# A fused Fourier filter and MLP on one core: twiddles put into the first and last DFT tables, and batch 0 worked by channel halves with most of its last stage in later slots

## The chip, the cores and the metric

The kernel runs on one core of a Trainium2 chip. The metric is device time in microseconds (us) from one launch; the time given for a kernel is the median of several runs on the same chip. Engines are named as in the profile: PE (TensorE), DVE (VectorE), ACT (ScalarE), POOL (GpSimd) and SP (SyncE, which here only issues DMAs).

## The reference, cut to what matters

```python
# x: 8 x 3008 x 256, filt_r and filt_i: 1505 x 256, w_in: 256 x 2048, w_out: 2048 x 256
X = np.fft.rfft(x, axis=1)
y = np.fft.irfft(X * (filt_r + 1j * filt_i)[None], n=3008, axis=1)
t = y.reshape(8 * 3008, 256)
h = t @ w_in
out = (0.5 * h * (1 + erf(h / sqrt(2)))) @ w_out
```

## The kernel before, in words

**The Fourier part.** 3008 is 47 x 64. A position n is written 64*n1 + 32*h + w, with n1 of 0..46, h of 0..1 and w of 0..31. Only 24 values k1 of the first transform are computed, since x is real. There are four stages: a DFT over n1 (table T1), a DFT over the 64 values (h, w) with the twiddle of each k1 (table T2), the product with the filter F, the inverse over 64 (T3, and T3i with real and imaginary parts turned), and the inverse over 47 (T4). T2 and T3 hold one 128x128 matrix for each of the 24 k1.

**Batch 0** goes first, alone, on the chip's own memory (functions c1 to c4). c1 multiplies x by T1 (16 groups; each is copied out of PSUM by DVE or ACT, L327 and L325). c1t transposes it to b_sb. c2 multiplies by T2, and DVE multiplies the PSUM result by F into p (L569; the last of the twelve is cut in two, L574). c3 multiplies by T3, and ACT copies it to vt_sb. c3t transposes vt_sb into d_sb (8 copies on DVE), and c4 multiplies by T4c and writes y_sb, the ring that the MLP reads (16 copies, 14 on ACT and 2 on DVE). The tables are made on the way by iotas on POOL, angles on DVE, sines on ACT, and matmuls with eye and swap. Each filter value is needed in both halves of the 128 partitions; dup_filters copies it (L137), two calls on DVE, one on ACT, nine on POOL. warm_up (L319) puts matmuls of ones into PE's queue between the steps.

**Batches 1 to 7** pass through HBM between the stages. fold (L109, L110) makes sums and differences of the two h on DVE, s1 (L429) is stage 1 with one table T1s for all positions, its result goes to R1 in HBM by SP's queue and comes back by r1, s2 (L456) and s2_out (L467) are stage 2 and the filter product with Fu (a second arrangement of F, made by move_filters, L130), s3 (L487) goes to R2, r2 reads it, and s4 (L514) multiplies by T4a. T4a, T2p, U and their factors are made on POOL and PE during the first tiles (table_2_parities, table_u_pick, table_4_rows, weights_4, table_4_factors, table_4_all).

**The MLP** runs over 47 tiles of 512 positions. mm1 (L640) makes 128x512 of h by two matmuls, and ACT applies Gelu into g_sb (L643). mm2 is mm2_first for tiles 0 to 2 (L656) and mm2_seven after that, which does seven products of sums instead of eight (L714; the sums on DVE, L685, L691, L696).

**What sets the order.** Each engine does its instructions in the program's order. After batch 0 the main loop runs over slots, 16 to a tile; slot s issues what was put there by put(slot, ...), then the mm2 matmuls of that slot, then one mm1. Tile 0's mm2_first starts in slot 10, so slots 0 to 9 hold ten mm1 and what is put there (fold in slots 0, 1, 5, 8; s1 in slots 4, 8, 11, 13). PSUM has eight banks: while batch 0 is worked, w (2), m (1) and n (5); in the main loop h (3), o (2) and f (3). An s1 takes three f banks and one lent from o or h. A DMA on POOL's or SP's queue waits for the one eight before it on that queue.

Of the kernel before, what the change touches and what calls it, by code (L numbers as in the profile page):

```python
# [10 lines left out]
ALU = mybir.AluOpType  # L11
# [20 lines left out]
class _Mix:  # L32
    def __init__(self, ctx, tc, x, filt_r, filt_i, w_in, w_out, out):
# [22 lines left out]
        self.T1 = c.tile([2 * NA, 96], BF16, name="T1")  # L56
        self.T2p = c.tile([128, K1, 2, 2, 16], BF16, name="T2p")
        self.xs = c.tile([128, 4, 256], BF16, name="xs")
        self.U = c.tile([128, 2, 2 * HB], BF16, name="U")
        self.T4c = c.tile([96, NA, 2], BF16, name="T4c")  # L60
# [5 lines left out]
        self.T4a = f[0:96, 4096:7168].rearrange("p (w m) -> p w m", w=HB)  # L66
# [54 lines left out]
    def move_filters(self, m0, m):  # L121

        for c in (3, 2, 1, 0):
            for q in range(2):
                for e in range(2):
                    o, k = 32 * c + 16 * q, 6 * c + m0
                    for t in ((0, 1),) if c or m0 == 0 else ((0,), (1,)):
                        t = slice(t[0], t[-1] + 1)
                        i = self.F[32 * q + e:32 * q + 32:2, t, k:k + m, :]
                        self.nc.sync.dma_start(  # L130
                            out=self.Fu[o:o + 16, t, e ^ q, m0:m0 + m, :].rearrange("p t m c -> p t (m c)"),
                            in_=i.rearrange("p t m c -> p t (m c)"))

    def dup_filters(self, eng, k0, k):
        for k in range(k0, k0 + k, 2):
            o, i = (self.F[r:r + 64, :, k:k + 2, :].rearrange("p t a b -> p t (a b)") for r in (64, 0))
            (eng.copy if eng is self.nc.scalar else eng.tensor_copy)(out=o, in_=i)  # L137
# [32 lines left out]
    def table_1(self, g):  # L170

        nc, ts = self.nc, self.nc.vector.tensor_scalar
        col = lambda name: g.tile([128, 1], FP32, name=name)
        off = g.tile([128, 2, K1], FP32, name="off")
        nc.vector.memset(off[:, 0, :], 0.25)
        nc.vector.memset(off[:, 1, :], 0.5)
        h, n1, hs, hc = col("h"), col("n1"), col("hs"), col("hc")
        ts(out=h, in0=self.p, scalar1=float(NA), scalar2=None, op0=ALU.is_ge)
        nc.vector.scalar_tensor_tensor(out=n1, in0=h, scalar=-float(NA), in1=self.p, op0=ALU.mult, op1=ALU.add)
        ts(out=hs, in0=h, scalar1=2.0 * PI, scalar2=None, op0=ALU.mult)  # L180
        ts(out=n1, in0=n1, scalar1=1.0 / NA, scalar2=None, op0=ALU.mult)
        ts(out=hc, in0=h, scalar1=-2.0 * PI, scalar2=2.0 * PI, op0=ALU.mult, op1=ALU.add)
        self.table_2_rows(g)
        w, r = g.tile([128, 2, K1], FP32, name="w1"), g.tile([128, 2, K1], FP32, name="r1")
        nc.vector.scalar_tensor_tensor(out=w, in0=self.k48, scalar=n1, in1=off, op0=ALU.mult, op1=ALU.add)
        ts(out=r, in0=w, scalar1=RND, scalar2=-RND, op0=ALU.add, op1=ALU.add)
        nc.vector.tensor_tensor(out=w, in0=w, in1=r, op=ALU.subtract)
        for q, s in enumerate((hc, hs)):
            nc.scalar.activation(out=self.T1[:, 48 * q:48 * q + 48], in_=w[0:2 * NA].rearrange("p a b -> p (a b)"),
                                 func=AF.Sin, scale=s[0:2 * NA])  # L190

    def table_2_rows(self, g):


        v = self.nc.vector
        ts = v.tensor_scalar
        col = lambda name, dt=FP32: g.tile([128, 1], dt, name=name)
        ri_i, m_i = col("ri_i", I32), col("m_i", I32)
        ts(out=m_i, in0=self.pi, scalar1=1, scalar2=None, op0=ALU.logical_shift_right)
        ts(out=ri_i, in0=self.pi, scalar1=1, scalar2=None, op0=ALU.bitwise_and)  # L200
        self.n2, self.ri = col("n2"), col("ri")
        v.tensor_copy(out=self.n2, in_=m_i)
        v.tensor_copy(out=self.ri, in_=ri_i)
        ts(out=self.n2, in0=self.n2, scalar1=1.0 / self.S, scalar2=None, op0=ALU.mult)
        ts(out=self.ri, in0=self.ri, scalar1=-0.25, scalar2=TURNS + 0.25, op0=ALU.mult, op1=ALU.add)

    def table_2_angle(self, g, h):


        v = self.nc.vector  # L210
        ts = v.tensor_scalar
        w = self.gen
        if h == 0:
            col = lambda name: g.tile([128, 1], FP32, name=name)
            jn = g.tile([128, NB], FP32, name="jn")
            ts(out=jn, in0=self.jj, scalar1=self.n2, scalar2=self.ri, op0=ALU.mult, op1=ALU.add)
            n6, self.n12 = col("n6"), col("n12")
            ts(out=n6, in0=self.n2, scalar1=6.0, scalar2=None, op0=ALU.mult)
            ts(out=self.n12, in0=self.n2, scalar1=12.0, scalar2=None, op0=ALU.mult)
            v.scalar_tensor_tensor(out=w[:, 0:6], in0=self.kk.unsqueeze(2).to_broadcast([128, 6, NB]), scalar=self.n2,  # L220
                                   in1=jn.unsqueeze(1).to_broadcast([128, 6, NB]), op0=ALU.mult, op1=ALU.add)

            self.T1c = g.tile([2 * NA, 96], BF16, name="T1c")
            v.tensor_copy(out=self.T1c.rearrange("p (k h r) -> p k h r", h=2, r=2),
                          in_=self.T1.rearrange("p (h r k) -> p k h r", h=2, r=2))
            ts(out=w[:, 6:12], in0=w[:, 0:6], scalar1=n6, scalar2=None, op0=ALU.add)
        else:
            ts(out=w[:, 12:24], in0=w[:, 0:12], scalar1=self.n12, scalar2=None, op0=ALU.add)
        k = slice(12 * h, 12 * h + 12)
        ts(out=self.gen_s.bitcast(I32), in0=w[:, k].bitcast(I32), scalar1=15, scalar2=None,  # L230
           op0=ALU.logical_shift_left)

    def signs(self, g):

        set_ = self.nc.vector.memset
        self.turn = [g.tile([128, 1], FP32, name=n) for n in ("turn_r", "turn_i")]
        for t, s in zip(self.turn, (-1.0, 1.0)):
            set_(t, s)
            for lo in (32, 96):
                set_(t[lo:lo + 32], -s)  # L240

        self.wtc = g.tile([128, 1], FP32, name="wtc")
        set_(self.wtc, 2.0)
        set_(self.wtc[0:4], 1.0)

    def weights_4(self, g):


        ts = self.nc.gpsimd.tensor_scalar
        h, q, self.wt, self.wts = (g.tile([128, 1], FP32, name=n) for n in ("h48", "q48", "wt", "wts"))  # L250
        ts(out=h, in0=self.p, scalar1=48.0, scalar2=None, op0=ALU.is_ge)
        ts(out=q, in0=h, scalar1=-48.0, scalar2=-4.0, op0=ALU.mult, op1=ALU.add)
        self.nc.gpsimd.tensor_tensor(out=q, in0=self.p, in1=q, op=ALU.add)
        self.nc.gpsimd.tensor_tensor(out=q, in0=q, in1=q, op=ALU.mult)
        ts(out=q, in0=q, scalar1=16.0, scalar2=-1.0, op0=ALU.is_equal, op1=ALU.mult)
        ts(out=self.wt, in0=q, scalar1=2.0, scalar2=None, op0=ALU.add)
        ts(out=h, in0=h, scalar1=-2.0, scalar2=1.0, op0=ALU.mult, op1=ALU.add)
        self.nc.gpsimd.tensor_tensor(out=self.wts, in0=self.wt, in1=h, op=ALU.mult)

    def unit_matrices(self, g, cols):  # L260
        ts = self.nc.vector.tensor_scalar
        self.eye, self.swap = (g.tile([128, 128], BF16, name=n) for n in ("eye", "swap"))
        sg, to = (g.tile([128, 1], FP32, name=n) for n in ("sg", "to"))

        ts(out=sg, in0=self.ri, scalar1=8.0, scalar2=-8.0 * TURNS - 1.0, op0=ALU.mult, op1=ALU.add)
        self.nc.vector.tensor_tensor(out=to, in0=self.p, in1=sg, op=ALU.add)
        ts(out=self.swap, in0=cols, scalar1=to, scalar2=sg, op0=ALU.is_equal, op1=ALU.mult)
        ts(out=self.eye, in0=cols, scalar1=self.p, scalar2=None, op0=ALU.is_equal)

    def table_2_sin(self, h):  # L270
        k = slice(12 * h, 12 * h + 12)
        self.nc.scalar.activation(out=self.T2[:, k, 0, :], in_=self.gen_s.bitcast(I32), func=AF.Sin,
                                  scale=2.0 * PI / 2.0 ** 32)

    def table_2_swap(self, h):
        t2 = self.T2[:, 12 * h:12 * h + 12]
        for i in range(2):
            ps = self.bank("ps_sw", "n")
            self.nc.tensor.matmul(ps[:, 0:384], lhsT=self.swap, rhs=t2[:, :, 0, 32 * i:32 * i + 32],
                                  start=True, stop=True)  # L280
# [760 lines left out]
```

## Time and profile before

| | |
|---|---|
| median of 3 runs | 733.68 us (733.53 to 733.91) |
| span of the profiled execution, first to last instruction | 732.0 us |
| PE busy | 713.6 us (97%) |
| DVE busy | 597.0 us (82%) |
| ACT busy | 576.5 us (79%) |
| POOL busy | 286.2 us (39%) |
| granted TensorE clock | 0.999 mean |
| first mm1 matmul (L640) | 37.30 us |
| first mm2 matmul (L656) | 44.02 us |

The span is what the profile sees of one execution; the runs are timed around it, so they are a little longer (1.7 us here). The profile's timeline gives for each engine the start of a group of like instructions, the time that it covers, the line, the operation with output and input, and how many; a bracket gives idle time before it and what ended it. Busy PE time is modelled, and a busy PE isn't a PE at its peak, but a wait that the view of waits puts on PE is one.

### The profile page before, as it was taken

What the parts mean: (1) busy time and instruction counts of PE and PEld (TensorE: products, weight loads), DVE (VectorE), ACT (ScalarE), POOL (GpSimd) and SP (SyncE); (2) the same over time, 40 slices, a digit from 0 to 9 for tenths busy, and PEclk for the clock granted to TensorE, in tenths of its full rate; (3) what the DMA queues carried; (4) which work ended last, traced back from release to release, by engine and by line L of the source; (5) the groups of instructions that cost most, each with busy time, mean ns of one, the idle gap of its engine ahead of it and who ended that gap; (6) DMA issues with size and microseconds to landing.
All of it is one profiled execution on the core that took longest, in us unless ns stands there. A gap on an engine that the chain in (4) does not pass through costs nothing.

```text
span 732.0 us, 22073 instructions
## 1 busy us (share of the span) xinstructions
PE 713.6 (97%) x9016; PEld 505.9 (69%) x9165; DVE 597.0 (82%) x1091; ACT 576.5 (79%) x1050; POOL 286.2 (39%) x546
## 2 busy tenths in 40 slices
PE   7999999999999999999999999999999999999997
PEld 4846675676777666666677667666677767777776
DVE  8975698899878998798976999779988897775666
ACT  7997778688877888778887788877888788877773
POOL 7853377864223452135511364115531121121121
PEclk9999999999999999999999999999999999999999
DMA  9886544765355553646535455355545442411011
GB/s 158 160 173 161 155 89 123 201 124 100 88 169 143 120 112 107 178 99 134 128 107 162 114 132 119 97 149 151 110 102 135 141 117 84 114 47 42 30 59 59
DMA packets 81254, 87.72 MB, mean 120 GB/s; under 512 B 13393, under 2 KB 61137, under 8 KB 81153
## 3 DMA queue, kind: packets, MB, share of 16 engines
q0 software_dynamic: 22288, 39.50, 24.3%
q1 hardware_dynamic: 58449, 46.62, 23.8%
q8 instruction: 71, 1.16, 0.7%
q14 instruction: 30, 0.25, 0.1%
q10 hardware_dynamic: 416, 0.20, 0.1%
HBM read 54.00 MB, written 46.66 MB: 138 GB/s over the span
## 4 chain that ended last, share of the span: by engine, by line
PE 86%; DVE 4%; DMA 4%; issue 2%; POOL 2%; ACT 1%; DVEq 0%; POOLq 0%; ACTq 0%
PE ps_o L714 38%; PE ps_h L640 38%; PE ps_s L514 3%; PE ps_o L656 2%; PE ps_s L429 2%; PE ps_s L487 2%; DMA x_sb<-in_x_dram 2%; PE ps_s L456 2%; DVE s_sb L685 1%; DMA w_out_sb<-in_moe_w_out_dram 1%; POOL F L137 1%; DMA F<-in_filt_i_dram 1%; ACT g_sb L643 1%; DVE p L467 1%; POOL x_sb L92 1%
## 5 line engine op out<-in xcount | busy, mean ns | idle before, releaser
L643 ACT ACTIVATE g_sb<-ps_h 128x512 f16<-128x512 f32 x752 | 446.4, 601 | 139.9 <-PE ps_h L640 115.5
L640 PE MATMUL ps_h<-y_sb,w_in_sb 128*128 128x512 bf16 (+3 forms) x1455 | 415.0, 365 | 1.5 <-DVE p L467 0.7
L761 POOL DMA_DIRECT2D out_dram<-ost x231 | 131.4, 575 | 388.0 <-DVE ost L743 361.3
L714 PEld LDWEIGHTS <-g_sb 128*128 128x128 f16 x2816 | 184.4, 98 | 80.7 <-issue 14.6
L640 PEld LDWEIGHTS <-w_in_sb 128*128 128x128 bf16 x1600 | 126.3, 98 | 8.3 <-issue 2.4
L714 PE MATMUL ps_o<-w_sums,g_sb 128*128 128x128 f16 x1408 | 121.7, 219 | 1.7 <-DVE g_sb L691 0.2
L714 PE MATMUL ps_o<-w_sums,s_sb 128*128 128x128 f16 x1408 | 121.2, 219 | 1.6
L714 PEld LDWEIGHTS <-s_sb 128*128 128x128 f16 x1408 | 95.1, 98 | 37.6 <-issue 2.5
L685 DVE TENSOR_TENSOR s_sb<-g_sb 128x1024 f16<-128x1024 f16 x176 | 116.4, 692 | 0.4 <-ACT g_sb L643 0.3
L714 PE MATMUL ps_o<-w_out_sb,g_sb 128*128 128x128 f16 x1408 | 113.7, 219 | 1.8
L467 DVE TENSOR_TENSOR p<-ps_s,Fu 128x1024 bf16<-128x1024 f32 x84 | 101.5, 1216 | 9.1 <-PE ps_s L456 6.5
L101 POOL DMA_DIRECT2D x_sb<-in_x_dram x156 | 79.4, 515 | 3.1 <-issue 1.6
L691 DVE TENSOR_TENSOR g_sb<-s_sb,g_sb 128x1024 f16<-128x1024 f16 x88 | 60.3, 687 | 1.5
L714 PE MATMUL ps_o<-w_out_sb,F 128*128 128x128 f16 x704 | 60.6, 219 | 0.9
L696 DVE TENSOR_TENSOR F<-g_sb 128x1024 f16<-128x1024 f16 x88 | 61.4, 697 | 0.0
L714 PEld LDWEIGHTS <-F 128*128 128x128 f16 x704 | 47.1, 98 | 14.6 <-issue 0.4
L736 DVE TENSOR_TENSOR t_sb<-t_sb,ps_o 128x256 f32<-128x256 f32 x44 | 18.4, 417 | 39.0 <-PE ps_o L714 38.6
L514 PEld LDWEIGHTS <-d_sb 96*128 96x128 bf16 x448 | 31.4, 97 | 26.8 <-issue 1.3
L325 ACT ACTIVATE F<-ps_s 128x512 bf16<-128x512 f32 x83 | 45.5, 607 | 0.1
L325 ACT ACTIVATE y_sb<-ps_s 128x376 bf16<-128x376 f32 x95 | 45.4, 478 | 0.1
L327 DVE CAST a_sb<-ps_s 128x512 bf16<-128x512 f32 x54 | 34.7, 684 | 12.0 <-PE ps_s L429 11.7
L743 DVE TENSOR_TENSOR ost<-t_sb,ps_o 128x256 f32<-128x256 f32 x86 | 32.1, 414 | 13.7 <-PE ps_o L714 13.7
(160 smaller groups left out, 589.2 us busy)
## 6 DMA issues: line engine op xcount, KB each, us to landing
out_dram<-ost POOLq DMA_DIRECT2D x127, 128.0 KB, 2.9
b_sb<-R SPq DMA_DIRECT2D x21, 512.0 KB, 5.1
R<-F SPq DMA_DIRECT2D x84, 128.0 KB, 2.5
d_sb<-R SPq DMA_DIRECT2D x56, 192.0 KB, 4.3
R<-a_sb SPq DMA_DIRECT2D x108, 96.0 KB, 2.2
x_sb<-in_x_dram POOLq DMA_DIRECT2D x48, 94.0 KB, 2.7
x_sb<-in_x_dram POOLq DMA_DIRECT2D x48, 48.0 KB, 2.8
x_sb<-in_x_dram POOLq DMA_DIRECT2D x12, 188.0 KB, 5.0
```

Of the source, the lines that this page charges most:

```text
L101: self.nc.gpsimd.dma_start(out=xt[64 * v + to:64 * v + to + m, h, 4 * c:4 * c + 4 * n, :], in_=xv[h][at:at + m, w:w + 4 * n, :])
L325: self.nc.scalar.activation(out=out, in_=in_, func=AF.Copy, scale=1.0 if scale is None else scale)
L327: self.nc.vector.tensor_copy(out=out, in_=in_)
L467: v(out=w[:, a], in0=ps.unsqueeze(2).to_broadcast([128, 2, 2, 256]), in1=f.unsqueeze(1).to_broadcast([128, 2, 2, 256]), op=ALU.mult)
L514: nc.tensor.matmul(ps[:, 94 * i:94 * i + 94], lhsT=d[:, (grp % 2) * 4 + i, 128 * half:128 * half + 128], rhs=self.T4a[:, 4 * grp + i, 0:2 ...
L640: nc.tensor.matmul(ps[:, o:o + n], lhsT=w[:, dc], rhs=self.ring[:, dc, off:off + n], start=(dc == 0), stop=(dc == 1))
L643: nc.scalar.activation(out=self.st["g", t][:, jc, :], in_=ps, func=AF.Gelu)
L685: self.nc.vector.tensor_tensor(out=self.st["s", t][:, i:i + 2], in0=a, in1=b, op=ALU.subtract)
L691: self.nc.vector.tensor_tensor(out=a21[:, k], in0=self.st["s", t][:, k, 0], in1=a22[:, k], op=ALU.add)
L696: self.nc.vector.tensor_tensor(out=self.s4_sb[:, k], in0=a12[:, k], in1=s2[:, k], op=ALU.subtract)
L714: nc.tensor.matmul(ps[:, (m + 1) % 2, sub, :], lhsT=a[:, i, 128 * sub:128 * sub + 128], rhs=b[:, i], start=i == 0, stop=i == 7)
L761: eng.dma_start(out=out, in_=tile_[lo - r0:lo - r0 + n])
```

## The change

The positions' twiddle moves out of the second and third tables into the first and the last. T1 becomes a table for each w (94 x 32 x 96), with the sum and the difference of the two h in it; T2 and T3 become one 128x128 matrix for all k1; T4 is a table for each w (96 x 32 x 94), made by 32 transposes of T1 and used by all batches. T1s (for s1) becomes a table for each of 16 positions, T2p and U are small. So the POOL tables in the first tiles go, s1 is 16 matmuls of 256 columns with 16 weights instead of 8 of 512 columns, R2 is written in pieces of one 256-vector and read by one DMA per part instead of two, and c3 uses one T3 for the eight matmuls of a unit.

Batch 0 is worked in twelve units of four k1 and one channel half. c1t, c2, c3 and c3t are done for each half; all of half 0 is finished first. Of the 16 c4 only four are done before the main loop: (0,0) and (1,0) between the last units, (0,1) and (1,1) right before the loop. The other twelve go to slots 2 to 25, copied out by DVE. Four c3t copies of half 0 are on ACT; of half 1 one is split between DVE and ACT, three are on DVE. dup_filters does two pieces on DVE, one on ACT, five on POOL, and SP sends the last eight k1 by DMA. move_filters is cut in three, the third in slot 28. The Gelu table of ACT is loaded in the middle of c1.

The diff, cut to its core ("-" before, "+" after):

```diff
+    def table_1_angle(self, w, n):
+        self.nc.vector.scalar_tensor_tensor(
+            out=b[:, w], in0=self.ww[:, w].unsqueeze(2).to_broadcast([128, n, K1]), scalar=self.first,
+            in1=self.kk.unsqueeze(1).to_broadcast([128, n, K1]), op0=ALU.add, op1=ALU.mult)
+        for r in range(2):
+            ts(out=a[:, r, w], in0=b[:, w], scalar1=1.0 / self.S, scalar2=TURNS + 0.25 + 0.25 * r,
+               op0=ALU.mult, op1=ALU.add)
+        ts(out=i, in0=i, scalar1=15, scalar2=None, op0=ALU.logical_shift_left)
+    def table_1_sin(self, w, n):
+        self.nc.scalar.activation(out=t, in_=a, func=AF.Sin, scale=2.0 * PI / 2.0 ** 32)
+    def table_1_odd(self, w, n, eng):
+        t = self.T1[:, w:w + n].rearrange("p w k a r -> p a (w k) r")
+        self._evac(t[:, 1], t[:, 0], eng, self.sign[0:2 * NA])
+    def table_3(self):
+        self.nc.tensor.transpose(ps[:, 0:128], self.T2, self.eye)
+        self._evac(self.T3[:, 0], ps[:, 0:128], "act")
+        for r in range(2):
+            self._evac(to[:, r], of[:, 1 - r], "act", self.turn[r])
+    def table_4(self, i, eng):
+        for w in range(8):
+            self.nc.tensor.transpose(ps[0:96, 2 * NA * w:2 * NA * w + 2 * NA],
+                                     self.T1[:, 8 * i + w].rearrange("p k a r -> p (k a r)"), self.eye[0:2 * NA, 0:2 * NA])
+        self._evac(self.T4[:, 8 * i:8 * i + 8, 0:2 * NA], ps[0:96, 0:16 * NA].rearrange("p (w m) -> p w m", w=8),
+                   eng, self.wt[0:96])
...
+    def send_filters(self, k, n):
+        self.nc.sync.dma_start(out=o, in_=i)
...
     def s1(self, b, c):
-        for i in range(2):
+        for i in range(4):
             for d in range(2):
                 for v in range(2):
-                    nc.tensor.matmul(ps[i][v][64 * d:64 * d + 64, :], lhsT=self.T1s[64 * v:64 * v + NA],
-                                     rhs=x[d][64 * v:64 * v + NA, 2 * i:2 * i + 2, :], start=True, stop=True)
+                    nc.tensor.matmul(ps[i // 2][v][64 * d:64 * d + 64, 256 * (i % 2):256 * (i % 2) + 256],
+                                     lhsT=self.T1s[64 * v:64 * v + NA, 4 * c + i],
+                                     rhs=x[d][64 * v:64 * v + NA, i, :], start=True, stop=True)
...
+    def c3(self, h, k, eng):
+        for i in range(4):
+            for t in range(2):
+                self.nc.tensor.matmul(ps[:, 128 * i:128 * i + 128], lhsT=w[:, t, 128 * i:128 * i + 128],
+                                      rhs=self.T3[:, t], start=t == 0, stop=t == 1)
+    def c4(self, u, half, eng, tag):
+        d = self.st[0, "d", half, u // 2]
+        ps = self.bank("ps_c4", tag)
+        for i in range(4):
+            self.nc.tensor.matmul(ps[:, 94 * i:94 * i + 94], lhsT=d[:, 4 * (u % 2) + i, :],
+                                  rhs=self.T4[:, 4 * u + i, 0:2 * NA], start=True, stop=True)
+        self.y_out(0, u, half, ps, eng)
...
+    for w, n in ((0, 8), (8, 8)):
+        m.table_1_angle(w, n)
+        m.table_1_sin(w, n)
+        m.table_1_odd(w, n, act)
+    for c in range(4):
+        for i, (u, h) in enumerate(order if c < 3 else [(0, 0), (1, 0), (0, 1), (1, 1)]):
+            m.c1(2 * c + u, h, (dve if c == 0 or i % 2 else act))
+        if c == 0:
+            m.table_1_angle(16, 16)
+            m.table_1_sin(16, 16)
+            m.table_1_odd(16, 16, dve)
+            m.table_2(g)
+            m.warm_up(3)
+            m.table_4(0, act)
+        if c == 1:
+            m.table_2_sin()
+            m.table_4(1, dve)
+            m.warm_up(2)
+        if c == 2:
+            nc.scalar.activation(out=g.tile([128, 1], FP32, name="warm"), in_=m.p, func=AF.Gelu)
+            m.table_4(2, dve)
+            m.table_4(3, dve)
+            m.warm_up(1)
+    m.dup_filters(nc.vector, 0, 0)
+    m.c1t(0, 0, (dve, act))
+    m.dup_filters(nc.scalar, 0, 4)
+    m.dup_filters(nc.vector, 1, 0)
...
+    m.c2(0, 0)
+    m.table_3()
+    m.c1t(1, 0, (act,))
+    m.c2(1, 0)
+    units = [(0, 0), (1, 0), (0, 4), (1, 4), (0, 8), (1, 8), (0, 12), (1, 12), (0, 16), (0, 20), (1, 16), (1, 20)]
+    turns = {0: (0, 8), 2: (1, 8), 5: (0, 16), 7: (1, 16)}
+    for i, (h, k) in enumerate(units):
+        if i in turns:
+            m.c1t(*turns[i], (act,))
+        if i + 2 < 12:
+            m.c2(*units[i + 2])
+        if i < 10:
+            m.warm_up(2)
+        m.c3(h, k, (act,) if i < 11 else (dve, act))
+        if i in (9, 10):
+            for j in range(2):
+                m.c3t(0, 2 * (i - 9) + j, (act,))
+            m.c4(0, 0, act, "n") if i == 9 else m.c4(1, 0, act, "n")
...
+    m.c3t(1, 0, (dve, act))
+    m.c3t(1, 1, (dve,))
+    m.c4(0, 1, dve, "h")
+    m.c4(1, 1, act, "o")
+    m.c3t(1, 2, (dve,))
+    m.c3t(1, 3, (dve,))
...
+    for u, slots in enumerate(((2, 3), (6, 7), (16, 17), (19, 21), (22, 23), (24, 25))):
+        for h in range(2):
+            put(slots[h], m.c4, u + 2, h, dve, "f")
+    put(15, m.table_u)
+    put(18, m.move_filters, 1)
+    put(28, m.move_filters, 2)
```

The left-out table_2 is 20 small DVE instructions on 1 to 256 columns, table_2_sin two sines. In the built program the order on DVE before the first product with F is: the first two angle tables, eye, four c1 copies, the third angle table, the odd half of T1, table_2, two c1 copies, one T4 copy, two c1 copies, two T4 copies, two c1 copies, a filter copy, half a c1t copy, a filter copy.

## The prediction

> **What bounds the kernel now.** I read the table of waits of PE first, over the whole span and again from 37 us to 150 us. Columns: who waited for whom, us in total, times, longest us. All but the first-tile waits are gone once the main loop runs:
>
> ```profile
> PE ps_h L640 <- DVE p L467: 0.7, 1, 0.7
> PE ps_o L656 <- DMA w_out_sb<-in_moe_w_out_dram: 0.3, 1, 0.3
> PE ps_h L640 <- ACT g_sb L643: 0.3, 1, 0.3
> PE ps_o L714 <- DVE g_sb L691: 0.2, 1, 0.2
> ```
>
> So from about 44 us to the end the kernel is a row of matmuls without gaps, and only two things move its time: when that row begins, and what is added to it. Then I read the timelines of DVE, ACT and PE from 0 to 60 us (start, time covered, line, operation, count), to see what sets the beginning.
>
> ```profile
> 6.73 1.02 DVE L327 CAST y_sb<-ps_c 128x384 bf16<-128x384 f32 x2
> ...
> 14.38 0.42 DVE L137 COPY F<-F 64x1024 bf16<-64x1024 bf16 x1 [0.23 <-DMA F<-in_filt_i_dram]
> ...
> 15.80 12.67 DVE L569 TENSOR_TENSOR p<-ps_c,F 128x1024 bf16<-128x1024 f32 x11
> 28.40 1.27 DVE L574 TENSOR_TENSOR p<-ps_c,F 128x512 bf16<-128x512 f32 x2
> 30.16 0.42 DVE L327 CAST vt_sb<-ps_c 128x256 bf16<-128x256 f32 x1 [0.49 <-PE ps_c L587]
> 31.34 5.56 DVE L327 COPY d_sb<-ps_c3t 96x1024 bf16<-96x1024 bf16 x8 [0.75 <-PE ps_c3t L602]
> 36.82 1.06 DVE L329 TENSOR_SCALAR y_sb<-ps_c 128x376 bf16<-128x376 f32 x2
> 37.80 0.68 DVE L109 TENSOR_TENSOR xs<-x_sb 111x1024 bf16<-111x1024 bf16 x1
> ```
>
> DVE carries the prologue: tables and c1 copies to 15.80, the filter products without a gap to 29.67, the c3t copies to 36.90.
>
> ```profile
> 30.46 1.28 ACT L900 ACT_TABLE_LOAD   x1
> 31.76 0.20 ACT L900 ACTIVATE warm<-p 128x1 f32<-128x1 f32 x1
> 32.46 5.53 ACT L325 ACTIVATE y_sb<-ps_c 128x376 bf16<-128x376 f32 x14 [0.50 <-PE ps_c L616]
> ```
>
> ACT copies the c4 results beside it. On PE the first mm1 and the first mm2 are at 37.30 and 44.02:
>
> ```profile
> 37.30 1.94 PE L640 MATMUL ps_h<-y_sb,w_in_sb 128*128 128x512 bf16 x7
> ...
> 44.02 0.60 PE L656 MATMUL ps_o<-w_out_sb,g_sb 128*128 128x256 f16 x4 [0.32 <-DMA w_out_sb<-in_moe_w_out_dram]
> ```
>
> The chart of the chain that ended last runs through POOL's filter copies and the load of w_out up to 44.02, but the idle time there is only 0.32 us: PE was ready at 43.7 by itself.
>
> **The change, step 1: the first product with F.** In the new program DVE has this queue before it, in order. It can begin its first c1 copy when T1's first part stands: DVE's columns and angles for 192 and 2x192 values (between the 48-column rows L185 to L187, 0.21 to 0.26 us each, and L220, L226, L230, 0.41 to 0.62), then two ACT steps of 384 elements of about 0.5; I take 6.3 us (before: 6.73). Then: ten c1 copies at a pitch of 0.47 (7.20 after 6.73): 4.7. The third angle table on 384 columns: L220 0.62, twice L226 0.41, L230 0.56: 2.0. DVE then stands in its queue for ACT's sine of 768 elements (L272, 0.84 us), 0.9, because the next instruction needs it. That is the odd half of T1, 94x768: between L312 (0.34 for 512 bf16) and L228 (0.61 for 768 f32); I take 0.5. table_2, 20 small dependent instructions: the 16 from L178 to L219 took 2.05 us (2.15 to 4.20), these are wider: 3.0 (2.4 to 3.6). Three T4 copies of 752 columns out of PSUM: no row has them; between 0.42 (512 columns, L327 b_sb) and 0.8 (one element in the time of the f32 copies); nearest is the c3t copy, 0.68 for 1024, so 0.55: 1.65. Two filter copies and half a c1t copy: 0.46, 0.42, 0.46: 1.3. Sum 14.05, so the first product starts at **20.3** instead of 15.80 (18.9 to 21.9). F isn't what it waits for: it had landed by 14.38, and its first piece is smaller now.
>
> **Step 2: the products.** Twelve of 128x1024 at a pitch of 1.13 (the x11 row): 13.6, as before (11 x 1.13 + 1.27 = 13.7). But now ACT is late for the second: after half a c1t copy (0.6) it has a filter copy (1.04), three T3 copies (0.55) and then the c1t copy of half 1 (1.04), so the second c2 is 1.2 later than DVE is free. The later c1t copies stand in ACT's queue between c3 copies and cost some 0.7 more in four places. Stalls 1.9 (0.7 to 2.6): the last product ends at 35.8 (before 29.68).
>
> **Step 3: the tail.** Before, 7.6 us went from the last product to the first mm1, with 8 c3t copies and 16 c4. Now only part of it is left, but in a chain on ACT. About when the last product ends, ACT has copied the last c3 of half 0; PE transposes (0.6 and a hand-over, 0.8), and ACT's queue is then: four c3t copies of 1024 at a pitch of 0.93 (b_sb rows: 17.73 to 18.63, 19.77 to 20.67): 3.7; two c4 copies at 0.40 (14 in 5.53): 0.8; one c3 copy 0.57 and half a one 0.35. 6.2 with the transposes, and the last of these frees vt_sb of half 1. Then in a row c3t (0.6), its halves on DVE and ACT (0.42 beside 0.60), c4 (0.3), its copy on ACT (0.48), with hand-overs of 0.1 to 0.2: 2.7. With the 0.6 between the end of the last product and the first of these: 9.5 (8.2 to 10.3). First mm1 at **45.3**, 8.0 later.
>
> **Step 4: slots 0 to 9.** Before, 6.7 us from the first mm1 to the first mm2 (37.30 to 44.02). An s1 needs three f banks. In the new order two c4 take f banks in slots 2 and 3, and their DVE copies stand behind two c3t copies (1.1 left at the first mm1) and four fold instructions at a pitch of 0.72: 1.1 + 2.9 + 2 x 0.53 = 5.0. So s1 in slot 4 starts 5.0 after the first mm1 (before: 39.16, 1.9 after), and PE stands, with all mm1 queued behind it. Then s1's DVE copies (1.28), a fold (1.4) and two more c4 copies (1.06) hold the s1 of slot 8 until 8.6; s1 (0.65) and two slots' mm1 (0.43 each) follow. First mm2 at **+9.7** (7.5 to 11), at 55.0 instead of 44.0. w_out isn't late: POOL has five filter copies (0.99 each) instead of nine, and its load needs the 8.0 us of its row.
>
> **Step 5: what is added to the row.** Eight c4 in slots 16 to 25: PE's pitch for the four matmuls of an s4 is 0.17, so 1.35. Gone are the factor matmuls of T4 (0.38). s1, 28 times, has 16 matmuls with 16 weights instead of 8; s2 and s3 have 32 with 32, and take 0.66 and 0.67 of PE's row (median of 21 each), against 0.65 for s1 (28; one lies from 115.71 to 116.36), so 0 to 0.5 in all; I take 0.05. The POOL tables that go cost PE at most the waits above on DVE, 0.9. DVE's eight copies (4.2) and weight sums (3.1) fill slots 16 to 25 (8.7), where DVE was idle 4.87 us at a stretch. R2's pieces of 512 B and the third move_filters on SP lie in slack: an r2 of the same pieces landed in 4.3 us, and 13 slots lie between two s3. Sum **+1.0** (0 to 1.5).
>
> **Sum.** 55.0 - 44.0 + 1.0 = 12.0 on a span of 732.0 gives 744.0; the runs lie 1.7 above the span, so **745.7 us**. With all low ends: 18.9 + 13.6 + 0.7 + 8.2 + 7.5 = 48.9, or +4.9: 738.6. With all high ends: 21.9 + 13.6 + 2.6 + 10.3 + 11 = 59.4, +15.4 + 1.5: 750.6, and the clock below on top.
>
> **A rule against the change.** The granted clock is 1.00 in every 5 us of the prologue, where PE's longest wait is 1.4. The new order leaves PE idle for about 3 us while DVE and ACT make the third part of T1 (warm_up comes behind it in the queue), and 2 us in the tail. If the clock fell to half there, the tail's PE steps (0.6, 0.3, 0.6) and a few before would double: 1 to 2 us, 747.4. The Trainium skill, "TensorE: Matmul & The Clock Gate", section "What's actually happening", says that the array's clock halves after an idle window of about 3.4 us and comes back after a busy one. By that rule the gap is just under the window, so I give it one chance in four, inside the range.
>
> **The rivals.** (a) *The prologue gets shorter, since work leaves it.* If DVE's table work lay beside other work as it does now (first product still at 15.80) and the tail kept only one c3t, one c4 and their copies, mm1 would start near 33 and w_out would be awaited at about 41.5, where mm2 would begin: -2.5 + 1.0, 732.2, and 731.5 without the DVE waits. For it: 12 of 16 c4 do leave the tail. Against it: DVE's queue sums to 14 us, and ACT's tail is a chain. It decides if the first product is before 17. Chance 0.08 for faster; 0.04 for a time within 0.2%. (b) *Only the start of the products is late*, with step 4's DVE queue hidden behind ACT's Gelu (ten at 0.52 and two s1 copies were nearly the bound before): without step 4 and the stalls of step 2, 740.8. Chance 0.17. (c) *ACT and DVE at the high ends, or the clock halved for long*: 750 to 755, chance 0.13. (d) The forecast, 742 to 750: 0.58. That the change doesn't do what it says is excluded by the built order.
>
> A measurement of this kernel tells about 0.2% (1.5 us) from no change. Faster 0.08, same 0.04, slower 0.88. Range 738.5 to 752.
>
> **What would show it.** First product on DVE near 20.3, a DVE wait for ACT before the odd half of T1, last product at 36, ACT without idle time from 37 to 42.6, first mm1 at 45, PE waiting for DVE before the s1 of slots 4 and 8, first mm2 near 55, and the row after that as long as before plus 1. A first product before 17, or a first mm2 before 47, would make it wrong.

## The result, and the profile after

The changed kernel takes **758.37 us** (median of 4 runs, 755.86 to 758.85) against 733.79 for the kernel before on the same chip (733.53 to 734.27): ratio 1.0326, 95% interval 1.0309 to 1.0342. The forecast was 745.7 with 752.0 as its upper end: the sign was right, the size about half. The profiled execution has a span of 755.9, which is 11.9 more than the 744.0 forecast for it. Five landmarks, in us from the span's start, divide it as the prediction's steps do (products end: the last product of batch 0 with F on DVE; row: from the first mm2 to the end of the span):

| | first product | products end | first mm1 | first mm2 | row | span |
|---|---|---|---|---|---|---|
| before | 15.80 | 29.67 | 37.30 | 44.02 | 688.0 | 732.0 |
| forecast | 20.3 | 35.8 | 45.3 | 55.0 | 689.0 | 744.0 |
| after | 22.82 | 40.54 | 50.27 | 59.69 | 696.2 | 755.9 |
| miss of each step | 2.5 | 2.2 | 0.2 | -0.3 | 7.2 | 11.9 |

So the tail and the slots came out close to their forecast, two steps were over 2 us short, and one, the row, failed. First the timelines of the profile after, with the lines that answer to those of before: DVE, then PE.

```profile
12.14 0.42 DVE L304 TENSOR_SCALAR T<-T,sign 94x768 bf16<-94x768 bf16 x1 [1.97 <-ACT T L205]
...
22.82 1.23 DVE L470 TENSOR_TENSOR p<-ps_c,F 128x1024 bf16<-128x1024 f32 x1
24.96 2.56 DVE L470 TENSOR_TENSOR p<-ps_c,F 128x1024 bf16<-128x1024 f32 x2 [0.92 <-PE ps_c L469]
```

```profile
12.79 0.80 PE L274 MATMUL ps_t<-eye,T 94*96 94x94 bf16 x8 [3.76 <-ACT T L300]
...
46.78 1.05 PE L496 MATMUL ps_c3t<-eye,vt_sb 128*128 128x128 bf16 x16 [1.94 <-ACT vt_sb L300]
...
48.77 1.71 PE L496 MATMUL ps_c3t<-eye,vt_sb 128*128 128x128 bf16 x16
50.27 1.91 PE L533 MATMUL ps_h<-y_sb,w_in_sb 128*128 128x512 bf16 x4
...
59.69 0.60 PE L549 MATMUL ps_o<-w_out_sb,g_sb 128*128 128x256 f16 x4
...
106.21 1.11 PE L360 MATMUL ps_s<-b_sb,T2p 64*32 64x256 bf16 x16 [5.26 <-ACT F L300]
```

The brackets are idle time and what ended it. DVE's wait for the third sine was forecast at half this size, PE's wait for ACT in the tail was forecast as it is. PE's gap of 3.76 had been put at about 3, and the 5.26 us at 106.21, deep in the main loop, were not forecast at all. The view of waits for 85 to 125 us gives the next steps of that last one, PE's wait for ACT (5.7 in two pieces) and ACT's own:

```profile
ACT F L300 <- DMA R<-F: 6.4, 1, 6.4
PE ps_s L360 <- ACT F L300: 5.7, 2, 5.3
```

ACT copies a result of s3 into v_sb, which lies in F's old place (hence the name F). It could not, because an R2 write that reads v_sb had not run (DVE, which copies the last part, waited 10.4 us for the same writes). SP's queue shows why (start, time covered, line, operation, count):

```profile
86.41 0.34 SPq L348 DMA_DIRECT2D b_sb<-R  x1
86.81 14.10 SPq L131 DMA_DIRECT2D Fu<-F  x20
101.01 1.27 SPq L654 DMA_DIRECT2D out_dram<-ost  x2
102.38 2.65 SPq L403 DMA_DIRECT2D R<-F  x4
```

The third move_filters of slot 28 stands behind an r1, then takes SP 14.10 us, and the first R2 writes, whose data ACT had copied by 86.8, follow at 102.38. Before, the first R2 writes ran 2.7 behind that r1, since no move_filters stood between them:

```profile
54.44 14.73 SPq L130 DMA_DIRECT2D Fu<-F  x20
...
72.13 0.33 SPq L444 DMA_DIRECT2D b_sb<-R  x1
...
74.87 2.46 SPq L497 DMA_DIRECT2D R<-F  x4
```

Last, the granted clock, in stretches of the span: the number ahead of the last two is the clock.

```profile
10.00:15.00 5.00, 2.21 (x18) 1.61 (x18) 2.96 (x21) 3.27 (x4) 2.85 (x6) 0.64 0.99 161
15.00:20.00 5.00, 4.09 (x43) 3.42 (x42) 4.40 (x10) 3.73 (x8) 4.94 (x11) 0.50 1.09 144
...
25.00:30.00 5.00, 5.00 (x40) 3.37 (x38) 3.63 (x3) 2.23 (x4) 4.96 (x10) 0.65 1.06 232
...
100.00:110.00 10.00, 4.21 (x45) 1.88 (x44) 1.82 (x2) 2.60 (x5) 0.00 (x0) 0.68 0.54 136
```

Read in stretches of 1 us, the clock is 1.00 up to 11 us, 0.72 in the next, 0.50 from 12 to 28, 0.75 in the next and 1.00 again, so I count a mean of 0.64 over 5 us as 3.6 us at half. With 5, 5 and 3.5 of the next stretches PE ran at half speed for 17 us of the prologue, and for 6.4 around the stall at 106. It did so once more, for 3.4 us from 49.0 to 52.4: the transposes at 48.77 took 1.71 instead of 1.05, the first four mm1 matmuls 1.91 (1.03 in e2).

### The profile page after: what moved, and what is told of

Same layout as the page of the kernel before. It is cut to its first block, busy times and chain, and to the rows that moved or that the text cites. A ratio compares the mean times of both kernels' runs of the same rounds, so it can differ in the third digit from the quotient of the medians.

```text
span 755.9 us, 22548 instructions
## 1 busy us (share of the span) xinstructions
PE 732.2 (97%) x9382; PEld 516.9 (68%) x9382; DVE 600.2 (79%) x1107; ACT 575.7 (76%) x1034; POOL 251.8 (33%) x488
## 4 chain that ended last, share of the span: by engine, by line
PE 89%; ACT 3%; DMA 3%; SPq 2%; POOL 1%; DVE 1%; issue 1%; DVEq 0%; POOLq 0%; ACTq 0%
PE ps_h L533 41%; PE ps_o L607 36%; PE ps_s L416 3%; PE ps_o L549 2%; PE ps_s L332 2%; SPq L131 2%; PE ps_s L360 2%; PE ps_s L391 1%; DMA x_sb<-in_x_dram 1%; ACT g_sb L536 1%; DMA R<-F 1%; DMA F<-in_filt_r_dram 1%; DMA d_sb<-R 1%; ACT d_sb L300 1%; ACT b_sb L300 1%
## 5 line engine op out<-in xcount | busy, mean ns | idle before, releaser
L533 PE MATMUL ps_h<-y_sb,w_in_sb 128*128 128x512 bf16 (+3 forms) x1600 | 447.8, 367 | 0.0
L300 ACT ACTIVATE y_sb<-ps_s 128x376 bf16<-128x376 f32 x95 | 45.4, 478 | 0.1
```

Of the source, the lines that this page charges most:

```text
L300: self.nc.scalar.activation(out=out, in_=in_, func=AF.Copy, scale=1.0 if scale is None else scale)
L533: nc.tensor.matmul(ps[:, o:o + n], lhsT=w[:, dc], rhs=self.ring[:, dc, off:off + n], start=(dc == 0), stop=(dc == 1))
```

## The experiments

The landmarks of every run's profile, and the medians of the runs (in brackets the ratio to the kernel before, with its interval):

| | first product | products end | first mm1 | first mm2 | row | span | runs |
|---|---|---|---|---|---|---|---|
| e1_early | 22.52 | 38.70 | 48.47 | 57.85 | 688.4 | 746.3 | 749.11 (1.0194 to 1.0237) |
| e2_warm | 22.34 | 38.76 | 47.89 | 57.19 | 697.0 | 754.2 | 756.27 (1.0288 to 1.0325) |
| e3_order | 20.25 | 38.44 | 48.18 | 57.59 | 695.8 | 753.4 | 755.48 (1.0284 to 1.0314) |
| e5_fold | 22.72 | 41.04 | 51.46 | 59.73 | 696.6 | 756.3 | 758.42 (1.0311 to 1.0356) |
| e4_sine | 21.18 | 37.44 | 47.36 | 56.60 | 688.3 | 744.9 | 747.03 (one run) |
| e6_fold | 23.04 | 41.27 | 50.40 | 57.81 | 689.3 | 747.1 | 748.94 (1.0182 to 1.0218) |
| e7_tail | 22.40 | 40.27 | 48.39 | 57.70 | 688.2 | 745.9 | 748.60 (1.0185 to 1.0219) |
| e8_all | 19.44 | 37.51 | 45.09 | 53.40 | 695.0 | 748.4 | 747.93 (1.0169 to 1.0212) |
| e9_best | 17.34 | 33.77 | 41.80 | 47.98 | 690.5 | 738.5 | 740.67 (1.0081 to 1.0112) |
| e10_cold | 17.95 | 34.38 | 42.41 | 48.59 | 690.3 | 738.9 | 740.91 (1.0084 to 1.0118) |
| f1_defer | 15.64 | 29.36 | 35.74 | 42.18 | 700.0 | 742.2 | 744.06 (1.0123 to 1.0153) |
| f2_defer | 15.53 | 29.36 | 35.65 | 43.26 | 690.7 | 734.0 | 736.28 (1.0020 to 1.0041) |
| e12_x_first | 17.31 | 33.74 | 41.78 | 47.95 | 689.2 | 737.1 | 739.05 (1.0054 to 1.0081) |

**e1_early: what stops the row.**

```diff
     m.move_filters(0)
+    m.move_filters(2)
...
-    put(28, m.move_filters, 2)
```

> One edit to the changed kernel: the third move_filters is put into SP's queue right after the first, ahead of the main loop, instead of in slot 28. Theory: its 20 DMAs (14.1 us of SP's queue from 86.81) hold up the R2 writes of batch 1 behind them, these hold v_sb, so ACT waits 6.4 us and PE 5.7, and the clock falls to half until 110.4. Then PE's 5.7 us wait for ACT at L360 is gone, the clock stays at 1.00 from 100 to 120, and the stretch from the first mm2 to the end falls from 696.2 to 689-690: 751 us (750 to 752.5). Rival, the R2 writes in pieces of 512 B (or s1's 16 weights) are the cause: R2 writes still late, PE waits near 100 again, 757 to 759.

The row falls from 696.2 to 688.4, and PE's waits from 60 to 130 us sum to 0.2. SP's queue now:

```profile
25.69 27.84 SPq L131 DMA_DIRECT2D Fu<-F  x36
...
85.05 0.34 SPq L348 DMA_DIRECT2D b_sb<-R  x1
85.48 1.74 SPq L654 DMA_DIRECT2D out_dram<-ost  x2
87.31 3.36 SPq L403 DMA_DIRECT2D R<-F  x4
```

The R2 writes follow the r1 by 2.3 us. The pieces of 512 B and s1's 16 weights are still there and cost nothing to be seen, so the rival falls: the stall, and the half clock after it, were the place of twenty DMAs in a queue. The time is even lower than expected, by an earlier first mm1 (48.47). That part need not be the edit: the instructions on PE up to there are the same, but in this execution the clock came back at 23.2 us instead of 28.5 (its row is 0.68 for 20 to 25 us, then 1.00); in e6, which has this edit too, it came back at 29.3.

**e2_warm and e3_order: the start.**

```diff
         if c == 1:
+            m.warm_up(16)
             m.table_2_sin()
```

> One edit to the changed kernel: 16 more warm_up matmuls (0.22 us each) in PE's queue behind the c1 matmuls of w 8 to 15, where PE stands 3.76 us. Theory, the clock that fell to half after that idle time (0.64 in 10 to 15 us, 0.50 in 15 to 25) makes PE late for DVE and ACT: the granted clock stays 1.00 to 30 us, first product at 22.0 to 22.5 instead of 22.82, the stalls of 0.92 among the products shrink to 0.4 to 0.6, first mm1 1.5 to 2.5 earlier than 50.27, 756 us. Rival, DVE and ACT alone set the prologue: clock 1.00 but first mm1 within 0.4 of 50.27 and the time within 0.5 of 758.4.

First mm1 2.4 earlier, and the runs 2.1 lower (their ranges overlap). But the clock was not kept: it fell at 16.6 and was half until 23.4, 6.8 us instead of 17. Nor is all of the 2.4 shown to be this edit's: e1, without it, had its first mm1 1.8 earlier. What the profiles show is that the first mm1 comes earlier the shorter the clock is at half in the prologue: 50.27, 48.47 and 47.89 with 17, 10 and 7 us. Of the 2.4, 0.6 lies in the tail, where the clock stayed at 1.00 in this execution; the last transposes before mm1, 1.71 in the changed kernel, are here:

```profile
46.99 1.06 PE L496 MATMUL ps_c3t<-eye,vt_sb 128*128 128x128 bf16 x16
```

```diff
         if c == 0:
+            m.warm_up(3)
+            m.table_4(0, act)
             m.table_1_angle(16, 16)
             m.table_1_sin(16, 16)
-            m.table_1_odd(16, 16, dve)
             m.table_2(g)
-            m.warm_up(3)
-            m.table_4(0, act)
+            m.table_1_odd(16, 16, dve)
```

> One edit to the changed kernel: the first T4 copy goes ahead of the third sine on ACT, and table_2 (3.0 us of small DVE instructions) ahead of the odd half of T1 on DVE, so that the sine of 1.90 us lies beside them. Theory, the 1.97 us that DVE waits for the sine are on the path: the wait is gone, first product at 20.9 (20.5 to 21.5), first mm1 1.5 to 2.5 earlier, 756 us. Rival, the c1 copies behind it wait for T1 on PE instead: the idle time moves to the c1 copies, first product not before 22.3, time within 0.7 of 758.4.

The c1 copies behind the odd half start at 13.42 instead of 15.39, so the wait of 1.97 was whole on the path. The first product is at 20.25, 2.57 earlier; the other 0.6 goes with two filter copies that took 0.42 each instead of 0.54 and 1.13, which the edit doesn't explain. First mm1 2.1 earlier, the runs 2.9 lower. The products took 18.2 here: ACT had the second c1t copy ready 1.5 late, and the clock fell a second time.

**e4_sine: why the third sine takes 1.90 us.** On the base of e1.

```diff
-        t = self.T1.rearrange("p w k a r -> p a r w k")[:, 0, :, w:w + n]
+        t = self.T1[:, w:w + n].rearrange("p w k a r -> p (w k a r)")[:, 0:48 * n].rearrange("p (r w k) -> p r w k", r=2, k=K1)
...
-        t = self.T1[:, w:w + n].rearrange("p w k a r -> p a (w k) r")
+        t = self.T1[:, w:w + n].rearrange("p w k a r -> p (w k a r)").rearrange("p (a w) -> p a w", a=2)
```

> Base: the changed kernel with the third move_filters right after the first (749.1 us, first product 22.52, first mm1 48.47). In each part of T1 the sine and the odd half now write rows without a stride (the first half of the part's columns, then the second), so the table's entries are in other places than they should be; every instruction and its size stays. Theory, the sine takes 1.90 us for 768 and 1.05 for 384 because its output goes to every fourth column: 0.84 and about 0.5 as the sines of before took, first c1 copy 1.0 earlier, DVE's wait for the third sine 0.9 instead of 1.97, first product at 20.3 to 20.9. Rival, the input (int32, two rows) or the neighbours on the engines make the sine slow: 1.90 and 1.05 stay, first product 22.5.

ACT's timeline of the changed kernel, then of e4:

```profile
10.21 1.90 ACT L205 ACTIVATE T<-y_sb 94x768 bf16<-94x768 int32 x1 [2.59 <-DVE y_sb L199]
```

```profile
4.31 0.52 ACT L205 ACTIVATE T<-y_sb 94x384 bf16<-94x384 int32 x1 [2.29 <-DVE y_sb L199]
...
10.25 0.84 ACT L205 ACTIVATE T<-y_sb 94x768 bf16<-94x768 int32 x1 [3.56 <-DVE y_sb L199]
```

The same elements cost 0.84 written side by side and 1.90 written to every fourth column (384: 0.52 and 1.05). DVE's wait falls to 0.91 and the first product comes 1.34 earlier than in e1. One part of the expectation missed: the first c1 copy starts at 6.48, as in e1 (6.52), and not 1.0 earlier. So the first two sines, though half as long, did not hold it; the second DMA of x landed at 5.98, just before PE began c1 at 6.11, which would explain it but was not tested.

**e5_fold, e6_fold, e7_tail: slots and tail.** In e5 the first two folds leave slots 0 and 1; in e6 (base e1) they stand further ahead, behind the last product, with the loads of x and w_out moved ahead of them in the program; e7 (base e1) is the last edit below.

```diff
+    m.fold(1, 0)
+    m.fold(1, 1)
     m.c3t(1, 0, (dve, act))
...
+        if i == 11:
...
+            m.fold(1, 0)
+            m.fold(1, 1)
         m.c3(h, k, (act,) if i < 11 else (dve, act))
...
-                m.c3t(0, 2 * (i - 9) + j, (act,))
+                m.c3t(0, 2 * (i - 9) + j, (dve if j else act,))
```

> One edit to the changed kernel: the first two folds of batch 1 (four DVE instructions at 0.72) go ahead of the c3t copies of half 1, into the 4.34 us in which DVE is idle from 40.54. Theory, the s1 of slot 4 stands behind DVE's queue of c3t copies, folds and c4 copies: first mm1 as before at 50.3, the stretch from the first mm1 to the first mm2 falls from 9.4 to 6.5-7, 755.8 us. Rival, s1 is held by f banks or x of batch 1 and not by the folds: the stretch stays above 8.8 and the time within 0.7 of 758.4; or the folds wait for x and make the first mm1 later.

> Base as for e4_sine (749.1 us). The first two folds of batch 1 now stand in DVE's queue right after the last product, ahead of the copy of the last c3 half (in the run before they stood behind that copy, so they did not reach DVE's idle 4.3 us). Theory, step 4 is DVE's queue: first mm1 as before (48.5, within 0.3), from there to the first mm2 6.8 to 7.5 instead of 9.4, 747 us. Rival, x of batch 1 lands too late, or PE and the f banks hold s1 whatever DVE does: the stretch from first mm1 to first mm2 stays above 8.5 or the first mm1 is later by as much; within 0.7 of 749.1.

> Base as for e4_sine (749.1 us). Two of the four c3t copies of half 0 go from ACT (0.96 each) to DVE, which is idle there for 4.3 us. Theory, the tail from the last product to the first mm1 (9.8) is ACT's chain: it falls by 1.5 to 2.0, first mm1 at 46.5 to 47.0, 747.3 us. Rival, the chain through PE's transposes and hand-overs sets it: less than 0.6.

In e5 the edit missed its aim: the folds came behind the copy of the last c3 half, so DVE stayed idle for 4.33 us and the folds pushed the c3t copies: first mm1 1.2 later, first mm2 where it was. In e6 they run in the idle time, and the stretch from first mm1 to first mm2 falls from 9.4 to 7.4 (it is 9.3 in e2 and e7, whose clock stays at 1.00 there as e6's does): step 4 was DVE's queue. In e7 the tail falls from 9.8 to 8.1, but not all of that is the edit: with the clock at 1.00 to the first mm1, the tail is 9.1 without it (e2 and e6). So the two copies were worth 1.0 of ACT's chain, less than the 1.5 to 2.0 expected, and the half clock 0.6. Neither gain reached the median (748.9 and 748.6 against 749.1), and the first mm1 of e6 was later than e1's, not equal: in these profiles the products end at 41.27 and 40.27, not at 38.70, and the clock's rows for 25 to 30 us are 0.57 and 0.71 where e1 has 1.00. The spread of the runs (1.8 to 3.4 us) is of that size, so these two gains stand on the profiles alone.

**e8_all, e9_best, e10_cold, e12_x_first: all mends together.** e8 has e1's, e3's and e7's edits, one early fold, and beside them:

```diff
-            m.c1(2 * c + u, h, (dve if c == 0 or i % 2 else act))
+            m.c1(2 * c + u, h, (dve if (i < 2 if c == 0 else i % 2) else act))
...
-            m.table_4(1, dve)
-            m.warm_up(2)
+            m.table_4(1, act)
+            m.warm_up(16)
...
-            m.table_4(2, dve)
-            m.table_4(3, dve)
-            m.warm_up(1)
+            m.warm_up(8)
...
+        if i in (4, 8):
+            m.table_4(1 + i // 4, act)
+        elif i < 10:
             m.warm_up(2)
```

> All edits at once on the base of e4_sine: the first T4 copy ahead of the third sine and table_2 beside it, two of the first four c1 copies and the T4 copies of parts 2 to 4 on ACT (parts 3 and 4 in the place of warm_up in two units), more warm_up behind c1 (16 and 8), two c3t copies of half 0 on DVE, the first fold ahead of them. By the steps: first product 17.5 (22.52 less 2.3 for the order, 0.95 for the c1 copies and 1.7 for the T4 copies), clock 1.00 to 30 us so the products take 15.5 and end at 33.0, first mm1 40.7 (tail 9.7 less 2.0), first mm2 48.5, the row as in the base, 738 us (735 to 741). Rival, ACT becomes what the products wait for, since it gets four more copies: products longer than 17 and first mm1 not before 43.5; 741 to 745. Not below the 733.6 of the kernel before by either.

The clock stays at 1.00 to 60 us, the first mm2 is 4.45 earlier than in e1, and the row is 6.6 longer: the gain was given back, and the median of 747.93 is far above the 738 expected. SP's queue of e8 shows one place:

```profile
25.34 31.37 SPq L131 DMA_DIRECT2D Fu<-F  x36
56.81 6.07 SPq L342 DMA_DIRECT2D R<-a_sb  x12
```

The first s1 is copied by 50, but its R1 writes wait for the moves until 56.8. What e1 had put out of the way stood in the way again as soon as the loop began earlier. (PE's waits behind it that the profile names sum to 3.9 of the 6.6; the rest I could not place.) And DVE stopped 1.98 until 34.02 at a product whose filter piece SP sends by DMA (issued at 24.7, landed 33.93; the profile names a transpose on PE, but the matmul that this product reads was done by 32.3).

e9 changes this in e8:

```diff
-    m.move_filters(2)
+    m.move_filters(2, nc.gpsimd)
...
-    for h, k in ((1, 4), (0, 8), (1, 8), (0, 12), (1, 12)):
+    for h, k in ((1, 4), (0, 8), (1, 8), (0, 12), (1, 12), (0, 16), (0, 20), (1, 16), (1, 20)):
         m.dup_filters(nc.gpsimd, h, k)
-    for k in (16, 20):
-        m.send_filters(k, 4)
...
-    for u, slots in enumerate(((2, 3), (6, 7), (16, 17), (19, 21), (22, 23), (24, 25))):
+    for u, slots in enumerate(((14, 15), (16, 17), (18, 19), (20, 21), (22, 23), (24, 25))):
```

with m.warm_up(10) and m.warm_up(2) for the 16 and 8, ACT's second c1t copy ahead of its filter copy and T3, and w_out's load between the two halves of x; e10 has no m.warm_up(10), and e12 has w_out's load behind x.

> The changed kernel with all of e8's reorderings of tables and copies, less warm_up (10 and 2 instead of 16 and 8, since DVE waited 0.91 and 1.39 for c1 behind them), and the queues sorted anew: the third move_filters goes on POOL's queue, which is idle from 41 us on, instead of SP's; POOL copies the last four filter pieces instead of two DMAs of SP, whose landing stopped a product for 1.98; the load of w_out is ahead of half of x; one fold ahead of the c3t copies of half 1; the twelve late c4 in slots 14 to 25. Theory, in e8 SP's queue (36 DMAs of the moves to 56.7, the R1 writes behind them) had become the bound, and gave the gain in the prologue back in the row (695.0 instead of 688.4): R1 writes start with the first s1, the row takes 688.4 to 689.1 again, first product 17.5, first mm1 39 to 41, first mm2 46 to 48.5, 736 to 738.5 us. Rival, the traffic itself and not the queue is the bound (DMA engines busy all of 5 to 45 us): x or w_out land late, the row is again over 691 or the first mm2 after 50: 741 to 745.

> e9 without the ten warm_up matmuls behind c1, nothing else: PE is idle there for about 2.5 to 3 us. If the granted clock falls to half, this gives its price by itself: PE's steps in c1, c1t and the first products twice as long, first mm1 1 to 2 later and the time 1 to 2 us longer. Rival, the gap is too short for the clock, or PE is off the path: the same time within 0.5.

> As e9_best, but the load of w_out goes behind all of x again. In e9 the third fold waited 2.08 for x (behind w_out in POOL's queue and in the traffic), and PE 1.27 at the first mm2 for it. Theory: this wait goes, w_out lands at about 47 and holds the first mm2 (47.98) by less than 0.5: 739 to 739.8 us. Rival, w_out comes after 49 and the first mm2 waits as long as the fold did: 740.5 to 741.5.

e9: the R1 writes start at 45.4 with the first s1, the wait of 1.98 is gone, slots 0 to 9 take 6.2. At 740.67 it lies 2 above its range and just under the rival's: first mm1 at 41.8 instead of 41 at most, and a row of 690.5 instead of 689.1, where a fold waited 2.08 for x behind w_out. e12 puts w_out behind x again: the wait is gone and the time 1.6 lower, as expected. It is the best form of the change that I found, and still 5.1 us slower than the kernel before.

e10 is e9 without ten warm_up: the clock row for 10 to 15 us is 0.80 instead of 1.00, for 15 to 20 0.86, together 3.4 us at half, and every landmark from the first product on is 0.61 later. That is less than the 1 to 2 expected, and the runs overlap (0.24 apart), so only the profile tells these apart.

**f1_defer and f2_defer: one part alone, on the kernel before.** Two c3t copies go to ACT, twelve c4 to slots 14 to 25; in f1 w_out is also loaded ahead of half of x.

```diff
+    for u in range(2, 8):
+        for half in range(2):
+            put(10 + 2 * u + half, m.c4, u, (False, False), (half,), "f")
```

> One part of the change alone, on the kernel before: twelve of the sixteen c4 go into slots 14 to 25 with their copies on DVE, three of the eight c3t copies on ACT... two of them, to be exact (3 and 5), and w_out is loaded ahead of half of x so that it does not hold the first mm2. Theory, deferring buys little: the first mm1 is 2 to 3 earlier than 37.30 but s1 and the folds on DVE hold the first mm2 to 41.5-42.5 (44.02 before), and the twelve c4 cost PE 12 x 0.17 = 2.0 in a row that has no gaps: 733 to 734.5, no difference that can be told. Rival, the last stage is what the prologue waits for: first mm2 before 41, 730 to 731.5; or DVE's copies in the slots stop s1 and s2: above 735.

> As f1_defer, but the load of w_out stays behind all of x as in the kernel before: in f1 DVE waited 5.69 for x of batch 1 (the third fold), and PE 6.1 behind it, which hid what the deferral does. Theory, the first mm1 is about 1.5 earlier as in f1 (35.7), but the first mm2 cannot be before w_out has landed at 44.0, so the 1.5 are lost there, and the twelve c4 add 12 x 0.17 = 2.0 to the row: 735 to 736.3 us. Rival, the copies of the c4 lie in DVE's idle time and the row takes no more than before: 733.3 to 734.3; or better than before, under 733, if w_out comes earlier.

f1 measured its side edit and lies far above its range (744.06): DVE waited 5.69 us for x, PE 6.1 behind it, and the clock was half from 45 to 55. f2 is the clean one. The first mm1 is 1.65 earlier, and then:

```profile
43.26 0.60 PE L656 MATMUL ps_o<-w_out_sb,g_sb 128*128 128x256 f16 x4 [1.00 <-DMA w_out_sb<-in_moe_w_out_dram]
```

w_out sets the first mm2, 0.76 earlier than before, and the row is 2.7 longer: the twelve c4 are 2.0 of it (in the trace the next matmul starts 0.17 behind each), and PE waits 0.6 for DVE's copies of them near 57 us. Deferring the last stage makes the kernel before 2.3 us slower: of the 1.65 that the first mm1 gains, the wait for w_out leaves 0.76, and the twelve c4 now stand in a row on PE that has no gap. The other half of the change, the new tables, was not run alone.

## Why the prediction was right in sign and wrong in size, step by step

- **Step 1, first product (20.3, measured 22.82).** The queue on DVE was in the order given. The term mis-sized is ACT's sine: I took 0.84 from a row with the same number of elements, but not the same output stride. It took 1.90, so DVE's wait was 1.97 instead of 0.9 (e4, e3). The first two took 1.05 instead of 0.5 as well, but that cost nothing: the first c1 copy started at 6.43 (forecast 6.3), and at 6.48 with short sines (e4). The rest of the 2.5 is 0.6 of waits for c1 on a slow PE and a filter copy of 1.13 instead of 0.42.
- **Step 2, products (15.5, measured 17.7).** Stalls of 2.9 instead of 1.9, and a pitch of 1.24 instead of 1.13. The row of the kernel before, from which I took the pitch, gives 1.145 (28.40 less 15.80, by eleven), so 0.2 is a misreading. In e1, whose program is the same up to here but for one move_filters on SP's queue, the clock was back at 23.2 and the products took 16.2, with stalls of 1.8 and a pitch of 1.20. So 1.5 of the miss goes with the clock; why a product takes 1.20 here and 1.15 before stays open.
- **The rule on the clock.** PE's gap was 3.76 and the clock fell, to which I gave one chance in four, since I had put the gap just under the window. That the clock halves in an idle stretch agrees with the rule of the Trainium skill that was weighed ("TensorE: Matmul & The Clock Gate", section "What's actually happening"); a whole idle window of about 3.4 us is not what these traces show before each fall: here the clock fell at 11.4, 2.4 us into the gap, and it also fell with gaps of 2.68 (e10) and 1.82 (e2). What I had wrong beside the chance is the price: PE stayed slow for 17 us, where I had priced a few steps, and the first mm1 was 1.8 to 2.4 earlier in the profiles with 10 and 7 us at half (e1, e2).
- **Step 3, tail (9.5, measured 9.7), and step 4, slots (9.7, measured 9.4).** The mechanisms hold: ACT's chain (e7) and DVE's queue of c3t copies, folds and c4 ahead of s1 (e6). That the sizes came so close is in part luck. At a clock of 1.00 the tail is 9.1 (e2, e6), and the 0.6 on top is the second fall of the clock, which the sum left out. The terms of step 4 as written add up to 10.1, not 9.7 (8.6, 0.65 and twice 0.43), and the first half of s1 in slot 4 started 3.2 after the first mm1, its second half 4.45, instead of 5.0.
- **Step 5, the row (+1.0, measured +8.2).** The step that failed is "R2's pieces of 512 B and the third move_filters on SP lie in slack". I had weighed how long one DMA takes to land, not how long twenty hold the queue, although the trace of before has that row (20 DMAs, 14.73 us, at 54.44). Behind r1 in slot 28 these 14 us end (100.9) after the second s3 has begun (98.46), and v_sb has two buffers, both still waiting for their R2 writes. Without it the row is +0.4 (e1), or +1.2 with all twelve c4 in it (e12): the sum of the other terms holds.
- **The rivals.** (a) fell: the first product was never before 17. (b) fell: step 4 was real. (c) has its clock, but the stall in the row, 7 us, was in none of them.

The change is slower even with all of this mended (e12): against the kernel before, the first product is 1.5 later, the products take 2.6 longer, the tail 0.4, slots 0 to 9 are 0.5 shorter and the row 1.2 longer, 5.1 in sum.

## What to carry to other kernels

When a step that issues DMAs moves, count the time for which it holds its queue (number times the spacing of the issues in the trace), and look for the next entry of that queue whose buffer someone needs: here 20 issues of 0.7 us cost 7.8 us of the row. Take the duration of an instruction from a row with the same shape and stride, not only the same count. And a mend that wins in one stage is to be followed to the end of the span, since the queue behind it may not have moved.

## What the runs showed of the hardware

- The sine's strided output (e4): 2.3 times as long for 768, twice for 384, when each element goes to every fourth column. The odd half of T1 writes two neighbouring columns of each four and did not show this: 0.42 both ways on DVE (768), 0.61 and 0.62 on ACT (384).
- The clock fell with less idle time than I had thought needed: in e2 PE was idle 1.82 us (14.33 to 16.15) and the clock was half from 16.6. But the length of the gap alone does not decide: a gap of 1.94 in the tail was followed by a fall in the changed kernel and in e1, and by none in e2 and e6; one of 1.82 in e8 (to 21.58) did nothing.
- The clock came back at 23.2 (e1) and at 28.5 us (after) in two executions whose prologue on PE had the same instructions, and the first mm1 was 1.8 apart. Runs of the changed kernel spread over 3.0 us, those of the kernel before over 0.7; the fastest of the four has a mean clock of 0.989, the others 0.982 to 0.984.
- In these programs a row of DMAs on one queue goes on at the pace of the issues, 0.6 to 0.7 us each, until the ninth has to wait for the first to land: in e8 SP issued a DMA at 33.95, when the one eight before it had landed at 33.93.
